# A fused retention and mixture-of-experts kernel: attention in blocks of two head pairs, half a batch ahead, with all its casts on GpSimd

## The chip, the core and the metric

The kernel runs on one core of a Trainium2 chip. A core has five engines with queues of their own: TensorE (PE, matrix products, with weight loads PEld beside them), VectorE (DVE), ScalarE (ACT), GpSimd (POOL) and SyncE (SP, which here only issues DMA). The metric is the device time of one execution in microseconds (us), the median of the runs given. Times inside an execution come from one profiled execution, counted from the start of its span.

## What is computed

Per batch (8), head (8), with 576 positions and a head dimension of 64, a retention attention: scores of q and k, multiplied by a decay that is zero above the diagonal, times v. Its output, transposed to 4608 tokens of 512 features, goes through four experts of two layers, mixed by normalised weights.

```python
scores = scale * np.matmul(q, k.transpose(0, 1, 3, 2))
Dmat = np.where(rel >= 0, gamma[:, None, None] ** rel[None, :, :], 0.0)
ret = scores * Dmat[None, :, :, :]
x = np.matmul(ret, v)                      # then to [B*S, H*D]
...
p = domain_probs / (domain_probs.sum(-1, keepdims=True) + 1e-09)
for e in range(E):
    h = np.maximum(x @ w1[e], 0.0)
    out += p[:, e:e + 1] * (h @ w2[e])
```

## The kernel before

**Tokens and experts.** The 4608 tokens are worked in nine tiles of 512 (`t` = 0 to 8). A tile has 16 up groups (`up_group`, L352: eight matmuls of 512 columns into one PSUM tile `ph`, then on DVE relu times the mixing weight `pB` into `h`, L364; in tile 0 on ACT) and, from tile 1 on, 14 down products (`Down.product`, L433: 16 matmuls of 256 columns each into `pd`). The products are a Strassen-Winograd scheme for two halves (s = 0, 1) of the tile: seven products each, in the order 1, 4, 2, 5, 6, 3, 7. They need the sums s1, s2, s4 and the difference in `h` (`Down.sums`, L421 to L431), which DVE makes from SBUF operands, each in two instructions. s1 is read by product 5, s2 by 6, s4 by 3 and the difference by 7. Tile 0 has plain down products.

**Order.** The schedule is manual: each engine runs its instructions in program order. In each tile a counter `n` goes through 30 slots: 16 up groups and 14 products. After each one, `run(slots, n)` issues what was put into that slot. So a slot fixes only the place in each engine's queue; an engine other than PE may run ahead to it.

**Attention.** Batch b needs tokens 576 b to 576 b + 575. Its first 512 positions are worked in four head pairs (`Pair`, L233), its last 64 in `Rem` (L302). Decay is folded into q and k: k and q are multiplied by tables while they are cast to bf16 (k on DVE L241, q on GpSimd L245, v copied on ACT L249), then k and q are transposed by DMA from SP's queue (L254). `scores` (L268) makes 8 matmuls with 64 contraction rows (array tiling 64x128) into `s`, and DVE multiplies by the triangle into `sT` (L276). `kv` (L257) makes 8 matmuls with 64 output rows (128x64) into `kvp`, which ACT copies to the block-diagonal `sbd` (L266). `values` (L280) makes 3 full-array products of `sbd` and q (L284), then the scores and kv of the following pair, then 8 products of v and `sT` (L291, 128x64), and ACT copies `o` to the token tile `xt` (L298). For batches 2 to 7, `attention` puts this into the tile before the batch: casts in slots 2, 7, 12, 18, heads in slots 7, 11, 17, 22, 27. Batches 0 and 1 are worked another way (`Unit`) in and before tile 0.

**Buffers.** All PSUM tiles come from one ring of four buffers (L64), taken in turn. `raw1`, the f32 load of a pair, has one buffer: the next load waits until the casts have read it. `bfs` has two sets (pairs p and p + 2 share one), `sbd` one.

**Queues.** SP issues in order: the two transposes of a pair, the six loads of the next (`load_pair`, L73), the remainder's five loads (`load_rem`), the output stores (L470, L486). GpSimd issues in order: the loads of next tile's `pB` (L222, in up groups 3, 7, 11, 15, each after DVE's last read of the old one), q casts (L245, L309) and the second half of an output sum (L485).

Of the kernel before, what the change touches and what calls it, by code (L numbers as in the profile page):

```python
# [9 lines left out]
FP32 = mybir.dt.float32  # L10
BF16 = mybir.dt.bfloat16
# [3 lines left out]
MULT = mybir.AluOpType.mult  # L15
# [8 lines left out]
def kernel(  # L24
# [41 lines left out]
    def ring_tile(name, shape, dt=FP32):  # L66
        return ring.tile(shape, dt, tag="ring", name=name)
# [5 lines left out]
    def load_pair(t, b, p, eng=nc.sync):  # L73
        for n, src in srcs:
            for j in range(2):
                eng.dma_start(out=t[n][:, :, j, :],
                              in_=src[b, 2 * p + j, 0:SM, :].rearrange("(c p) d -> p c d", p=C))
# [10 lines left out]
    bfr = {n: const.tile([128, NP, 2, D], BF16, name=f"bfr_{n}") for n, _ in srcs}  # L88
    raw1 = {n: const.tile([128, NC, 2, D], FP32, name=f"raw1_{n}") for n, _ in srcs}
    bfs = [{n: const.tile([128, NC, 2, D], BF16, name=f"bf{i}_{n}") for n, _ in srcs} for i in range(2)]  # L90
    q1 = const.tile([128, 2, 2, 4, D], BF16, name="q1")
    raw2 = const.tile([128, 3, 2 * NC * D], FP32, name="raw2")
    sbd = const.tile([128, NP, NC, 128], BF16, name="sbd")

    w1_sb = [const.tile([128, NDC, F], BF16, name=f"w1_{e}") for e in range(E)]
# [131 lines left out]
    def xt_of(t):  # L227
        if t not in xt:
            xt[t] = xpool.tile([128, NDC, NT], BF16, tag="xt", name="xt")
        return xt[t]  # L230


    class Pair:  # L233
        def __init__(self, b, p):
            self.b, self.p = b, p
            self.bf = bfs[p % 2]

        def cast(self, raw, n):
            p = self.p
            if n == "k":  # L240
                nc.vector.tensor_tensor(  # L241
                    self.bf["k"], raw["k"],
                    gk[:, :, 2 * p:2 * p + 2].unsqueeze(3).to_broadcast([128, NC, 2, D]), op=MULT)
            elif n == "q":
                nc.gpsimd.tensor_tensor(  # L245
                    self.bf["q"], raw["q"],
                    gq[:, :, 2 * p:2 * p + 2].unsqueeze(3).to_broadcast([128, NC, 2, D]), op=MULT)
            else:
                nc.scalar.activation(self.bf[n], raw[n], Copy)  # L249

        def trans_dma(self):
            self.qkT = atp.tile([128, 2, NC, C], BF16, tag="qkT", name="qkT")
            for i, n in ((1, "k"), (0, "q")):
                nc.sync.dma_start_transpose(  # L254
                    out=self.qkT[:, i, :, :], in_=self.bf[n][:, :, :, :].rearrange("p c h d -> p (c h d)"))

        def kv(self):  # L257
            kvp = ring_tile("kvp", [128, NC, D])
            for c in range(NC):
                for j in range(2):  # L260
                    nc.tensor.matmul(kvp[64 * j:64 * j + 64, c:NC, :], lhsT=self.bf["k"][:, c, j, :],  # L261
                                     rhs=self.bf["v"][:, c, j, :].unsqueeze(1).to_broadcast([128, NC - c, D]),
                                     start=(c == 0), stop=(c == NC - 1), skip_group_check=True)
            for j in range(2):
                r = slice(64 * j, 64 * j + 64)
                nc.scalar.activation(sbd[r, self.p, :, r], kvp[r, :, :], Copy)  # L266

        def scores(self):  # L268
            self.sT = atp.tile([128, 2, NC, C], BF16, tag="sT", name="sT")
            s = ring_tile("s", [128, 2, NC, C])  # L270
            for c in range(NC):
                for j in range(2):
                    r = slice(64 * j, 64 * j + 64)
                    nc.tensor.matmul(s[:, j, c, :], lhsT=self.qkT[r, 1, c, :], rhs=self.qkT[r, 0, c, :],  # L274
                                     start=True, stop=True)
            nc.vector.tensor_tensor(  # L276
                self.sT[:, :, :, :].rearrange("p j c t -> p (j c) t"), s[:, :, :, :].rearrange("p j c t -> p (j c) t"),
                tri[:, :].unsqueeze(1).to_broadcast([128, 2 * NC, C]), op=MULT)

        def values(self, following=None):  # L280
            b, p = self.b, self.p
            o = ring_tile("o", [128, SM])
            for c in range(1, NC):
                nc.tensor.matmul(o[:, c * C:(c + 1) * C], lhsT=sbd[:, p, c - 1, :], rhs=self.qkT[:, 0, c, :],  # L284
                                 start=(c == 1), stop=False, skip_group_check=True)
            if following is not None:
                following.scores()
                following.kv()
            for c in range(NC):
                for j in range(2):  # L290
                    nc.tensor.matmul(o[64 * j:64 * j + 64, c * C:(c + 1) * C], lhsT=self.bf["v"][:, c, j, :],  # L291
                                     rhs=self.sT[:, j, c, :], start=False, stop=(c == NC - 1), skip_group_check=True)
            n0 = b * S
            a = 0
            while a < SM:
                t = (n0 + a) // NT
                z = min(SM, (t + 1) * NT - n0)
                nc.scalar.activation(xt_of(t)[:, p, n0 + a - t * NT:n0 + z - t * NT], o[:, a:z], Copy)  # L298
                a = z


    class Rem:  # L302
        def __init__(self, b):
            self.b = b

        def cast(self, q_engine=nc.gpsimd):
            nc.vector.tensor_tensor(
                bfr["k"], rawr["k"], gkr[:, :].unsqueeze(2).unsqueeze(3).to_broadcast([128, NP, 2, D]), op=MULT)
            q_engine.tensor_tensor(  # L309
                bfr["q"][0:R], rawr["q"][0:R],  # L310
                gqr[0:R].rearrange("p (g j) -> p g j", j=2).unsqueeze(3).to_broadcast([R, NP, 2, D]), op=MULT)
            nc.scalar.activation(bfr["v"], rawr["v"], Copy)

        def alloc_trans(self):
            self.kT = atp.tile([128, NP, 128], BF16, tag="kTr", name="kTr", bufs=1)
# [333 lines left out]
    for u in range(NU):  # L649
# [10 lines left out]
        if u == NU - 2:  # L660
            warm(2)
    mixing_weights()
    raw1u = {n: raw1[n][:, :, :, :].rearrange("p c j d -> p (c j d)") for n in "kqv"}
    bf1 = [{}, {}]
    for g in range(2):
# [24 lines left out]
    load_w1(3)  # L690
    load_v(2)
    load_w2(3)
    early.close()
    hp = ctx.enter_context(tc.tile_pool(name="hp", bufs=1))
    h = hp.tile([128, E * NFC, NT], BF16, name="h")


    def attention(slots, b, cast_at, head_at):
        add = lambda i, f: slots.setdefault(i, []).append(f)
        xs = [Pair(b, p) for p in range(NP)]  # L700
        add(head_at[0], xs[0].scores)
        add(head_at[0], xs[0].kv)
        for p in range(NP):
            add(head_at[p + 1], lambda p=p: xs[p].values(xs[p + 1] if p + 1 < NP else None))
        for p, c in enumerate(cast_at):
            x = xs[p]
            add(c, lambda x=x: [x.cast(raw1, n) for n in "kqv"])
            add(c, x.trans_dma)
            if p + 1 < NP:
                add(c, lambda p=p: load_pair(raw1, b, p + 1))  # L710
            elif b + 1 < B:
                add(c, lambda: load_pair(raw1, b + 1, 0))

    def remainder(slots, b, at):
        add = lambda i, f: slots.setdefault(i, []).append(f)
# [9 lines left out]
    def run(slots, i):  # L725
        for f in slots.get(i, []):
            f()
# [41 lines left out]
            run(slots, n)  # L769
            n += 1  # L770

    HK = KH // 2
    for t in range(1, n_nt):
        slots = {i - 32: f for i, f in slots.items() if i >= 32} if t == 1 else {}
        d = [Down(h, t, s) for s in range(2)]
        add = lambda i, f: slots.setdefault(i, []).append(f)
        for s in range(2):
            for i, which in enumerate((1, 2, 4, 3)):
                for lo in (0, KH // 2):
                    add(16 + 7 * s + i, lambda s=s, which=which, lo=lo: d[s].sums(which, lo, lo + KH // 2))  # L780
        if t == 1:
            rem_next = Rem(1)
            add(0, rem_next.cast)
            add(0, rem_next.trans_dma)
            add(5, rem_next.scores)
            add(7, rem_next.values)
        elif t < B:
            add(2, rem_next.scores)
            add(4, rem_next.values)
        if t + 1 < B:  # L790
            rem_next = Rem(t + 1)
            add(21, lambda t=t: load_rem(t + 1))
            add(26, rem_next.cast)
            add(26, rem_next.trans_dma)
        if t + 1 < B:
            attention(slots, t + 1, (2, 7, 12, 18), (7, 11, 17, 22, 27))
        run(slots, -1)
        n = 0
        for e in range(E):
            for i in range(4):  # L800
                up_group(h, t, e, i)
                run(slots, n)
                n += 1
        for s in range(2):
            for m in (1, 4, 2, 5, 6, 3, 7):
                d[s].product(m)
                run(slots, n)
                n += 1
# [30 lines left out]
```

## Time and profile before

| | us |
|---|---|
| median of 3 runs (541.2 to 541.92) | 541.65 |
| the profiled execution | 541.59 |
| its span | 539.9 |
| tile 1 to tile 2, first up matmul to first up matmul (84.42 to 142.69) | 58.27 |
| tiles 2 to 6, each | 57.81 |
| h eviction, DVE L364, mean | 1.222 |
| sT, DVE L276, mean | 1.217 |
| k cast, DVE L241, mean (lowest 0.677) | 0.907 |
| q cast, GpSimd L245, mean | 1.108 |
| v copy, ACT L249, mean | 0.629 |

The profile names instructions by line, engine, operation and the tiles they write and read. A group line has count, busy time, mean ns of one, and the idle time of the engine just before. In timelines a trailing bracket is idle time before the row and what released it. "Chain" is the sequence of work that ended last, followed back from the last instruction.

### The profile page before, as it was taken

The page shows a single profiled execution, that of the slowest core. Times are in us where ns is not written, and L with a number is a line of the kernel's source. Part 1 is how long each engine was busy: PE and PEld are TensorE (multiplying, and loading weights), DVE is VectorE, ACT ScalarE, POOL GpSimd, SP SyncE. Part 2 cuts the span into 40 slices and gives each one's busy share as a digit, 9 for nine tenths or more (in the row PEclk, how much of TensorE's full clock was granted, in tenths as well). Part 3 has the DMA queues.
Part 4 walks back from the last instruction along what each step waited for, and adds up shares of the span by engine and source line. Part 5 has one row for each costly group of instructions (what it writes and reads, how often), then busy time and mean ns, then how long its engine had stood idle before and what let it go on. Part 6 is the DMA issues. An engine that isn't in the chain of part 4 may idle for free.

```text
span 539.9 us, 10290 instructions
## 1 busy us (share of the span) xinstructions
PE 528.9 (98%) x4278; PEld 340.8 (63%) x4318; DVE 366.4 (68%) x484; ACT 112.3 (21%) x255; POOL 92.8 (17%) x126
## 2 busy tenths in 40 slices
PE   8999999999999999999999999999999999999997
PEld 4444554568645884488547864687458844884486
DVE  5425669987488757875689658764886677557764
ACT  4633551122111320223022111131112200000010
POOL 5734001120211120211112111202111100010000
PEclk9999999999999999999999999999999999999999
DMA  9999957865266725555287517652654211110001
GB/s 239 207 211 250 227 133 178 154 148 118 84 119 133 166 77 109 136 111 141 73 158 123 146 55 137 157 138 85 105 132 117 80 42 39 41 41 21 0 27 53
DMA packets 145119, 63.56 MB, mean 118 GB/s; under 512 B 124240, under 2 KB 135888, under 8 KB 145072
## 3 DMA queue, kind: packets, MB, share of 16 engines
q1 hardware_dynamic: 134752, 43.50, 35.9%
q0 software_dynamic: 10176, 19.27, 16.3%
q8 instruction: 34, 0.56, 0.5%
q10 hardware_dynamic: 144, 0.13, 0.1%
q14 instruction: 13, 0.11, 0.1%
HBM read 53.56 MB, written 9.51 MB: 117 GB/s over the span
## 4 chain that ended last, share of the span: by engine, by line
PE 92%; DVE 4%; ACT 1%; issue 1%; DMA 1%; SPq 0%; DVEq 0%
PE ph L358 45%; PE pd L450 37%; PE po L377 4%; DVE h L364 2%; PE kvp L261 1%; PE s L274 1%; PE o L291 1%; ACT qkT L518 1%; DMA raw_0q<-in_q_dram 1%; PE o L284 1%; DVE sT L541 0%; PE kvp L558 0%; PE pt L516 0%; PE s L539 0%; PE o L602 0%
## 5 line engine op out<-in xcount | busy, mean ns | idle before, releaser
L358 PE MATMUL ph<-xt,w 128*128 128x512 bf16 x1118 | 252.5, 379 | 3.3 <-DVE h L364 1.4
L358 PEld LDWEIGHTS <-w 128*128 128x128 bf16 x1152 | 110.9, 98 | 129.6 <-issue 1.9
L364 DVE SCALAR_TENSOR_TENSOR h<-ph,pB 128x1024 bf16<-128x1024 f32 x128 | 155.9, 1222 | 51.1 <-PE ph L358 50.9
L450 PEld LDWEIGHTS <-h 128*128 128x128 bf16 x1024 | 99.2, 98 | 14.1
L450 PEld LDWEIGHTS <-s 128*128 128x128 bf16 x768 | 74.7, 98 | 9.1
L450 PE MATMUL pd<-wx,h 128*128 128x256 bf16 x512 | 61.3, 273 | 0.0
L450 PE MATMUL pd<-wx,s 128*128 128x256 bf16 x512 | 61.2, 273 | 0.0
L222 POOL DMA_DIRECT2D pB<-pd x28 | 15.9, 568 | 168.5 <-DVE h L364 136.8
L266 ACT ACTIVATE sbd<-kvp 64x256 bf16<-64x256 f32 x48 | 18.2, 379 | 105.6 <-PE kvp L261 105.3
L485 POOL TENSOR_TENSOR ob<-v,p 128x256 f32<-128x256 f32 x15 | 10.9, 727 | 146.9 <-DVE v L482 97.6
L245 POOL TENSOR_TENSOR bf_q<-raw_q,gq 128x512 bf16<-128x512 f32 x24 | 26.6, 1108 | 27.0 <-DMA raw_q<-in_q_dram 15.1
L276 DVE TENSOR_TENSOR sT<-s,tri 128x1024 bf16<-128x1024 f32 x24 | 29.2, 1217 | 2.1 <-PE s L274 2.1
L450 PE MATMUL pd<-t2w,s 128*128 128x256 bf16 x256 | 30.6, 273 | 0.0
L450 PE MATMUL pd<-t4w,h 128*128 128x256 bf16 x256 | 30.6, 273 | 0.0
L450 PE MATMUL pd<-t3w,h 128*128 128x256 bf16 x256 | 30.6, 273 | 0.0
L467 DVE TENSOR_TENSOR u<-pd,p 128x256 f32<-128x256 f32 x16 | 6.8, 425 | 33.7 <-PE pd L450 33.7
L377 PE MATMUL po<-wx,h 128*128 128x512 bf16 x124 | 28.4, 379 | 0.3 <-issue 0.2
L458 ACT ACTIVATE p<-pd 128x256 f32<-128x256 f32 x16 | 6.1, 384 | 92.8 <-PE pd L450 88.7
L469 DVE TENSOR_TENSOR oa<-pd,u 128x256 f32<-128x256 f32 x16 | 6.8, 425 | 23.7 <-PE pd L450 23.7
L431 DVE TENSOR_TENSOR s<-h,s 128x1024 bf16<-128x1024 bf16 x32 | 22.6, 747 | 0.0
L429 DVE TENSOR_TENSOR h<-h 128x1024 bf16<-128x1024 bf16 x32 | 22.2, 735 | 0.0
L249 ACT ACTIVATE bf_v<-raw_v 128x512 bf16<-128x512 f32 x24 | 15.1, 629 | 33.5 <-DMA raw_v<-in_v_dram 33.5
(147 smaller groups left out, 390.8 us busy)
## 6 DMA issues: line engine op xcount, KB each, us to landing
pB<-pd POOLq DMA_DIRECT2D x28, 256.0 KB, 3.9
raw_k<-in_k_dram SPq DMA_DIRECT2D x48, 128.0 KB, 2.7
raw_q<-in_q_dram SPq DMA_DIRECT2D x48, 128.0 KB, 3.2
raw_v<-in_v_dram SPq DMA_DIRECT2D x48, 128.0 KB, 4.0
wx<-in_moe_w_dram POOLq DMA_DIRECT2D x4, 1024.0 KB, 15.4
out_dram<-oa SPq DMA_DIRECT2D x16, 256.0 KB, 2.1
out_dram<-ob SPq DMA_DIRECT2D x15, 256.0 KB, 2.0
w<-in_moe_w_dram POOLq DMA_DIRECT2D x3, 1024.0 KB, 15.1
```

The costliest lines, as they stand in the source:

```text
L222: eng.dma_start(out=pB[t, e], in_=pd[e:e + 1, t * NT:(t + 1) * NT].to_broadcast([128, NT]))
L245: nc.gpsimd.tensor_tensor(self.bf["q"], raw["q"], gq[:, :, 2 * p:2 * p + 2].unsqueeze(3).to_broadcast([128, NC, 2, D]), op=MULT)
L249: nc.scalar.activation(self.bf[n], raw[n], Copy)
L266: nc.scalar.activation(sbd[r, self.p, :, r], kvp[r, :, :], Copy)
L276: nc.vector.tensor_tensor(self.sT[:, :, :, :].rearrange("p j c t -> p (j c) t"), s[:, :, :, :].rearrange("p j c t -> p (j c) t"), tri[:, : ...
L358: nc.tensor.matmul(ph[:, f, :], lhsT=w1_sb[e][:, dc, fc * 128:(fc + 1) * 128], rhs=x[:, dc, :], start=(dc == 0), stop=(dc == NDC - 1))
L364: nc.vector.scalar_tensor_tensor(h[:, fk:fk + 2, :], ph, 0.0, pB[t, e][:, :].unsqueeze(1).to_broadcast([128, 2, NT]), op0=MAX, op1=MULT)
L377: nc.tensor.matmul(po[:, g, :], lhsT=h[:, e * NFC + fc, ns * 128:(ns + 1) * 128], rhs=wx[e // 2][:, (e % 2) * NFC + fc, :, :].rearrange("p ...
L429: nc.vector.tensor_tensor(h[:, l, self.b], h[:, l, self.a], h[:, l, self.b], op=SUB)
L431: nc.vector.tensor_tensor(self.alloc("s4")[:, l], h[:, r, self.a], self.s2[:, l], op=SUB)
L450: mm = nc.tensor.matmul(dst, lhsT=src[:, kk, tok], rhs=rhs(c), start=(start and c == 0), stop=(c == KH - 1), skip_group_check=True)
L485: nc.gpsimd.tensor_tensor(self.ob[:, HF:Dm], self.v, self.p5, op=ADD)
```

## The change

Batches 2 to 7 are worked by `Duo`, two head pairs at a time, and `block(new, old)`: the kv of the new two pairs, then the values of the old two (v and `sT` products first, then the `sbd` products), then the scores of the new two. So within a block the array tilings are 128x64, 128x128 and 64x128, in this order. The `sbd` copies and the `xt` copies take two pairs at once.

All casts of these batches, and of the remainders of batches 1 to 7, are on GpSimd: k, q, v in this order. In tile 0 the remainder's v cast moves from ACT to DVE. k and q are transposed into tiles of their own (two buffers for kT, four for qT), and v has four buffers, so that a pair's v and q outlive the next half batch.

The slots of tiles 1 to 8 are now one list, numbered through (30 per tile). Batches 2, 3 and 4 have places of their own; from batch 5 on, with g = 30 (b - 3): casts at g+3, +8, +15, +21, blocks at g+13 and g+33, remainder loads at +17, casts at +27, scores at +36, values at +38. Batch 2 has no old values in its first block, its last values stand alone in slot 27, and batch 3's first block again has no old ones; the last values of batch 7 are at slot 163, in tile 6. As before, tiles 7 and 8 have no head pairs; the remainder of batch 7 is now in tile 6.

Two buffers of tile 0 (`q1`, `raw2`) move into a pool that is closed after tile 0; the new tiles take its place.

```diff
+    class Duo:
...
+        def cast(self, p):
+            for n, eng, g in (("k", nc.gpsimd, gk), ("q", nc.gpsimd, gq)):
+                eng.tensor_tensor(bfs[p % 2][n], raw1[n],
+                                  g[:, :, 2 * p:2 * p + 2].unsqueeze(3).to_broadcast([128, NC, 2, D]), op=MULT)
+            nc.gpsimd.tensor_copy(bv[p], raw1["v"])
+            self.kT[p] = dpl.tile([128, NC, C], BF16, tag="kT", name="kT", bufs=2)
+            self.qT[p] = dpl.tile([128, NC, C], BF16, tag="qT", name="qT", bufs=4)
+            for t, n in ((self.kT[p], "k"), (self.qT[p], "q")):
+                nc.sync.dma_start_transpose(out=t, in_=bfs[p % 2][n][:, :, :, :].rearrange("p c h d -> p (c h d)"))
...
         def kv(self):
+            kvp = ring_tile("kvp", [128, 2, NC, D])
+            for i, p in self.pairs():
+                for c in range(NC):
+                    for j in range(2):
+                        nc.tensor.matmul(kvp[64 * j:64 * j + 64, i, c:NC, :], lhsT=bfs[p % 2]["k"][:, c, j, :],
+                                         rhs=bv[p][:, c, j, :].unsqueeze(1).to_broadcast([128, NC - c, D]),
+                                         start=(i == 0 and c == 0), stop=(c == NC - 1), skip_group_check=True)
             for j in range(2):
                 r = slice(64 * j, 64 * j + 64)
-                nc.scalar.activation(sbd[r, self.p, :, r], kvp[r, :, :], Copy)
+                nc.scalar.activation(sbd[r, self.ps, :, r], kvp[r], Copy)
...
+        def values(self):
+            o = ring_tile("o", [128, 2, SM])
+            for i, p in self.pairs():
+                for c in range(NC):
+                    for j in range(2):
+                        nc.tensor.matmul(o[64 * j:64 * j + 64, i, c * C:(c + 1) * C], lhsT=bv[p][:, c, j, :],
+                                         rhs=self.sT[p][:, j, c, :], start=(c == 0), stop=False, skip_group_check=True)
+            for i, p in self.pairs():
+                for c in range(1, NC):
+                    nc.tensor.matmul(o[:, i, c * C:(c + 1) * C], lhsT=sbd[:, p, c - 1, :], rhs=self.qT[p][:, c, :],
+                                     start=False, stop=(c == NC - 1), skip_group_check=True)
...
+    def block(new, old):
+        if new is not None:
+            new.kv()
+        if old is not None:
+            old.values()
+        if new is not None:
+            new.scores()
...
-        def cast(self, q_engine=nc.gpsimd):
-            nc.vector.tensor_tensor(
+        def cast(self, engine=nc.gpsimd):
+            engine.tensor_tensor(
                 bfr["k"], rawr["k"], gkr[:, :].unsqueeze(2).unsqueeze(3).to_broadcast([128, NP, 2, D]), op=MULT)
-            q_engine.tensor_tensor(
+            engine.tensor_tensor(
...
-            nc.scalar.activation(bfr["v"], rawr["v"], Copy)
+            engine.tensor_copy(bfr["v"], rawr["v"])
...
+    NS = 30
+    slots = {i - 32: f for i, f in slots.items() if i >= 32}
+    rem1 = Rem(1)
+    for at, f in ((0, rem1.cast), (0, rem1.trans_dma), (5, rem1.scores), (7, rem1.values)):
+        add(at, f)
+    old = None
+    for b in range(2, B):
+        g = NS * (b - 3)
+        cast_at, block_at, rem_at = {
+            2: ((1, 8, 13, 17), (13, 22), (14, 20, 25, 28)),
+            3: ((22, 27, 32, 37), (32, 42), (34, 40, 45, 47)),
+            4: ((42, 47, 52, 57), (52, 62), (53, 59, 65, 68)),
+        }.get(b, ((g + 3, g + 8, g + 15, g + 21), (g + 13, g + 33), (g + 17, g + 27, g + 36, g + 38)))
+        duos = [Duo(b, d) for d in range(2)]
+        for d in range(2):
+            if b == 3 and d == 0:
+                add(27, lambda old=old: block(None, old))
+                old = None
+            add(block_at[d], lambda new=duos[d], old=old: block(new, old))
+            old = duos[d]
+        for p, at in enumerate(cast_at):
+            add(at, lambda d=duos[p // 2], p=p: d.cast(p))
+            if p + 1 < NP:
+                add(at, lambda b=b, p=p: load_pair(raw1, b, p + 1))
+            elif b + 1 < B:
+                add(at, lambda b=b: load_pair(raw1, b + 1, 0))
...
+    add(NS * 5 + 13, lambda old=old: block(None, old))
```

More of the change, by code (lines that the diff above doesn't have):

```diff
@@ L90 @@
     bfs = [{n: const.tile([128, NC, 2, D], BF16, name=f"bf{i}_{n}") for n, _ in srcs} for i in range(2)]
-    q1 = const.tile([128, 2, 2, 4, D], BF16, name="q1")
-    raw2 = const.tile([128, 3, 2 * NC * D], FP32, name="raw2")
     sbd = const.tile([128, NP, NC, 128], BF16, name="sbd")
@@ L230, in xt_of @@
         return xt[t]
[L233 to L240, printed above, removed]
-                nc.vector.tensor_tensor(
[L242 to L255, printed above, removed]
-        def kv(self):
[L258 to L263, printed above, removed]
@@ new lines, with __init__, pairs @@
+    class Duo:
+        def __init__(self, b, d):
+            self.b, self.d = b, d
+            self.ps = slice(2 * d, 2 * d + 2)
+            self.qT, self.kT, self.sT = {}, {}, {}
+        def cast(self, p):
[7 more added lines that the diff above has]
+                nc.sync.dma_start_transpose(out=t, in_=bfs[p % 2][n][:, :, :, :].rearrange("p c h d -> p (c h d)"))
+        def pairs(self):
+            return enumerate((2 * self.d, 2 * self.d + 1))
+        def kv(self):
+            kvp = ring_tile("kvp", [128, 2, NC, D])
[5 more added lines that the diff above has]
+                                         start=(i == 0 and c == 0), stop=(c == NC - 1), skip_group_check=True)
@@ L264, in kv @@
             for j in range(2):
                 r = slice(64 * j, 64 * j + 64)
-                nc.scalar.activation(sbd[r, self.p, :, r], kvp[r, :, :], Copy)
+                nc.scalar.activation(sbd[r, self.ps, :, r], kvp[r], Copy)
         def scores(self):
[L269 to L293, printed above, removed]
+            for i, p in self.pairs():
+                sT = self.sT[p] = atp.tile([128, 2, NC, C], BF16, tag="sT", name="sT")
+                s = ring_tile("s", [128, 2, NC, C])
+                for c in range(NC):
+                    for j in range(2):
+                        r = slice(64 * j, 64 * j + 64)
+                        nc.tensor.matmul(s[:, j, c, :], lhsT=self.kT[p][r, c, :], rhs=self.qT[p][r, c, :],
+                                         start=True, stop=True)
+                nc.vector.tensor_tensor(
+                    sT[:, :, :, :].rearrange("p j c t -> p (j c) t"), s[:, :, :, :].rearrange("p j c t -> p (j c) t"),
+                    tri[:, :].unsqueeze(1).to_broadcast([128, 2 * NC, C]), op=MULT)
@@ new lines, in values @@
+        def values(self):
+            o = ring_tile("o", [128, 2, SM])
+            for i, p in self.pairs():
+                for c in range(NC):
+                    for j in range(2):
+                        nc.tensor.matmul(o[64 * j:64 * j + 64, i, c * C:(c + 1) * C], lhsT=bv[p][:, c, j, :],
+                                         rhs=self.sT[p][:, j, c, :], start=(c == 0), stop=False, skip_group_check=True)
+            for i, p in self.pairs():
+                for c in range(1, NC):
+                    nc.tensor.matmul(o[:, i, c * C:(c + 1) * C], lhsT=sbd[:, p, c - 1, :], rhs=self.qT[p][:, c, :],
+                                     start=False, stop=(c == NC - 1), skip_group_check=True)
+            n0 = self.b * S
@@ L297, in values @@
                 z = min(SM, (t + 1) * NT - n0)
-                nc.scalar.activation(xt_of(t)[:, p, n0 + a - t * NT:n0 + z - t * NT], o[:, a:z], Copy)
+                nc.scalar.activation(xt_of(t)[:, self.ps, n0 + a - t * NT:n0 + z - t * NT], o[:, :, a:z], Copy)
                 a = z
+    def block(new, old):
[5 more added lines that the diff above has]
+            new.scores()
     class Rem:
@@ L304, in __init__ @@
             self.b = b
-        def cast(self, q_engine=nc.gpsimd):
-            nc.vector.tensor_tensor(
+        def cast(self, engine=nc.gpsimd):
+            engine.tensor_tensor(
                 bfr["k"], rawr["k"], gkr[:, :].unsqueeze(2).unsqueeze(3).to_broadcast([128, NP, 2, D]), op=MULT)
-            q_engine.tensor_tensor(
+            engine.tensor_tensor(
                 bfr["q"][0:R], rawr["q"][0:R],
                 gqr[0:R].rearrange("p (g j) -> p g j", j=2).unsqueeze(3).to_broadcast([R, NP, 2, D]), op=MULT)
-            nc.scalar.activation(bfr["v"], rawr["v"], Copy)
+            engine.tensor_copy(bfr["v"], rawr["v"])
         def alloc_trans(self):
@@ L662 @@
     mixing_weights()
+    early.close()
+    hp = ctx.enter_context(tc.tile_pool(name="hp", bufs=1))
+    h = hp.tile([128, E * NFC, NT], BF16, name="h")
+    first = ctx.enter_context(ExitStack())
+    fpool = first.enter_context(tc.tile_pool(name="fpool", bufs=1))
+    q1 = fpool.tile([128, 2, 2, 4, D], BF16, name="q1")
+    raw2 = fpool.tile([128, 3, 2 * NC * D], FP32, name="raw2")
     raw1u = {n: raw1[n][:, :, :, :].rearrange("p c j d -> p (c j d)") for n in "kqv"}
@@ L692 @@
     load_w2(3)
[L693 to L712, printed above, removed]
     def remainder(slots, b, at):
@@ L770 @@
             n += 1
-    HK = KH // 2
+    first.close()
+    dpl = ctx.enter_context(tc.tile_pool(name="dpl", bufs=1))
+    bv = [bfs[0]["v"], bfs[1]["v"]] + [dpl.tile([128, NC, 2, D], BF16, name=f"v{i}") for i in range(2)]
+    NS = 30
[7 more added lines that the diff above has]
+        cast_at, block_at, rem_at = {
[3 rows of a table added]
+        }.get(b, ((g + 3, g + 8, g + 15, g + 21), (g + 13, g + 33), (g + 17, g + 27, g + 36, g + 38)))
[12 more added lines that the diff above has]
+                add(at, lambda b=b: load_pair(raw1, b + 1, 0))
+        rem = Rem(b)
+        add(rem_at[0], lambda b=b: load_rem(b))
+        for at, f in ((rem_at[1], rem.cast), (rem_at[1], rem.trans_dma), (rem_at[2], rem.scores), (rem_at[3], rem.values)):
+            add(at, f)
+    add(NS * 5 + 13, lambda old=old: block(None, old))
     for t in range(1, n_nt):
-        slots = {i - 32: f for i, f in slots.items() if i >= 32} if t == 1 else {}
         d = [Down(h, t, s) for s in range(2)]
-        add = lambda i, f: slots.setdefault(i, []).append(f)
         for s in range(2):
@@ L779 @@
                 for lo in (0, KH // 2):
[L780 to L798, printed above, removed]
+                    add(NS * (t - 1) + 16 + 7 * s + i,
+                        lambda s=s, which=which, lo=lo, d=d: d[s].sums(which, lo, lo + KH // 2))
+        n = NS * (t - 1)
         for e in range(E):
```

## The prediction

> **What bounds the kernel now.** I read the page first: busy shares, then the chain that ended last.
>
> ```profile
> PE 528.9 (98%) x4278; PEld 340.8 (63%) x4318; DVE 366.4 (68%) x484; ACT 112.3 (21%) x255; POOL 92.8 (17%) x126
> ...
> PE 92%; DVE 4%; ACT 1%; issue 1%; DMA 1%; SPq 0%; DVEq 0%
> ```
>
> TensorE (PE) is busy 98% and carries 92% of the chain, so a change pays only if it shortens PE's own sequence or PE's waits. Next, the table of stretches, one token tile each (us, then busy time of PE, PEld, DVE, ACT, POOL):
>
> ```profile
> 373.93:431.74 57.81, 57.40 (x469) 38.53 (x473) 41.78 (x51) 10.64 (x27) 9.69 (x11) 1.00 0.48 107
> 484.40:536.20 51.80, 51.69 (x348) 34.15 (x349) 33.05 (x41) 2.30 (x6) 2.18 (x3) 1.00 0.05 19
> ```
>
> A tile with one batch's attention between its expert matmuls (tiles 1 to 6) takes 57.81, one without 51.80: attention costs about 6 us a tile, six times. Clock 1.00 in both. Then the chain within one tile (start, length, what):
>
> ```profile
> 349.84 0.17 PE o L284 x3
> 350.01 0.33 PE s L274 x8
> 350.34 0.40 PE kvp L261 x8
> 350.74 0.23 PE o L291 x8
> 350.96 8.84 PE pd L450 x80
> ...
> 369.76 0.17 PE o L284 x3
> 369.93 0.34 PE o L291 x8
> 370.28 1.74 PE pd L450 x15
> ```
>
> The same eight o matmuls of L291 take 0.23 directly after kvp (same array tiling, 128x64) and 0.34 directly after L284 (full array): 0.11 is the price of the change of tiling. It shows at each one: s takes 0.33, though eight half-array matmuls side by side stream 4x128 columns, 0.22 at 0.0539 per 128 columns (16 matmuls of 512 in 3.45 elsewhere in the chain): 0.11 over; kvp 0.40 against 0.27: 0.13; the 80 pd behind it 8.84 against 8.73 (24.45/224 each): 0.11. I take 0.12 a change. Last, PE's timeline where it sits idle:
>
> ```profile
> 397.10 1.67 PE L358 MATMUL ph<-xt,w 128*128 128x512 bf16 x6 [0.20 <-DVE h L364]
> ```
>
> The four PSUM ring buffers set this: o, s, kvp follow ph 11, so ph 12 needs the buffer of ph 11, whose eviction (1.22) has just begun. The list of waits has six such, 1.4 us together.
>
> **PE, tiling changes.** The matmuls stay the same in number and shape; only their order changes. Before, per batch: scores and kv alone: 3 changes (into s, into kv, back); three pairs with a following one: 3 each (full to s, s to kv, o back); the last: 2. That is 14, times 6 = 84. After: block = kv of two pairs, then o of the old two (same tiling), sbd products (full), scores, back: 4 changes, eight or so per batch. Counted out with the special cases: 3+4+2 for batch 2 (its last values alone in slot 27), 3+4 for batch 3, 8 each for 4 to 7, and 2 for the last values: 50. Removed 34 x 0.12 = 4.1 us, all of it on the path, since PE waits for nothing there.
>
> **PE, the ring wait.** A block takes kvp, o, s, s from the ring. The first s needs the buffer of the ph before last, the second that of the last ph (DVE done at 1.3 after the block starts, PE there after kv 0.54+0.12, o 0.43, sbd 0.32+0.12, s 0.22+0.12: 1.9). Covered; the 1.4 goes. What is late next: the following ph needs kvp's buffer, evicted by two ACT operations of 64x512. No such row; 64x256 takes 0.38 and the L298 row of 128x448 0.54, so 0.59 each: 0.76 after the start plus 1.2 = 1.95, PE arrives at 2.05 to 2.1. Between 0 and 0.1 a block over 11 blocks with scores: 0 to 1.1 us; I take 0.3, since it should just fit. In slot-22 blocks the buffer is pd's, free 0.9 after its last product. sT (two of 1.22 on DVE) and xt are read a block or more later: covered by ten slots.
>
> **DVE and ACT lose the casts** (24 x 0.68 or more, and 24 x 0.63): off the path, credited nothing.
>
> **GpSimd gains them.** Uncontended rows: a k or q cast 1.04, a v copy 0.61 (L503): 2.7 a pair instead of one 1.04; 4 pairs and a remainder add some 9 us to 9.7 busy of 57: room. Queued behind a cast that waits for its load: the pB loads (needed a tile later) and the ob sum of L485 (its p5 is rewritten four products later, 7 us). Neither reaches PE. The Trainium skill, "GPSIMD Engine Reference", "4.1 Engine selection", speaks against this: elementwise work belongs on VectorE, GpSimd being about twice as slow for two inputs. Rows: 1.04 against 0.68, 1.5 times. By the rule a pair is 2x1.36+0.61 = 3.3 (an estimate), by the row 2.7; both fit, so the sum is the same.
>
> **The port.** DVE's Strassen sums read two SBUF operands, and so do the casts:
>
> ```profile
> 233.11 1.28 DVE L427 TENSOR_TENSOR s<-s,h 128x1024 bf16<-128x1024 bf16 x2
> ...
> 235.91 1.66 DVE L431 TENSOR_TENSOR s<-h,s 128x1024 bf16<-128x1024 bf16 x2
> ```
>
> ```profile
> 235.37 1.04 POOL L245 TENSOR_TENSOR bf_q<-raw_q,gq 128x512 bf16<-128x512 f32 x1 [1.68 <-DMA raw_q<-in_q_dram]
> ```
>
> (GpSimd's row is quoted from its own timeline.) The sums that started under the cast took 0.38 more, the cast kept its 1.04. "SBUF — State Buffer", "SBUF: two separate sides", calls it an exclusive lock, the later one blocked for the whole instruction. If bandwidth were shared, a cast would stretch too and cost DVE perhaps a half; by the lock each meeting costs DVE what is left of the cast, up to 1.04. I sum with the lock. First half of a steady tile: DVE frees after ph 15; pair 2 casts then. With the engines taking turns, s1 is done 2.3 later (due at 3.9), s2 at 5.2 (due 5.7), s4 6.5 (7.4), s3 7.8 (9.2). Second half, against pair 3, the ob sum and the remainder cast (6.1 of GpSimd together): s1 at 2.8 (due 5.2), s2 5.8 (7.0), s4 8.7 (8.7, second half 9.6), s3 10 (10.5). No wait, with half a us to spare. The h evictions read PSUM and one SBUF operand; beside casts they keep 1.22.
>
> **SP's queue.** Cycle of a pair now (start, length):
>
> ```profile
> 150.07 1.20 SPq L254 DMA_TRANSPOSE qkT<-bf_k  x1
> 151.36 1.23 SPq L254 DMA_TRANSPOSE qkT<-bf_q  x1
> 152.64 1.12 SPq L76 DMA_DIRECT2D raw_k<-in_k_dram  x2
> 153.81 1.44 SPq L76 DMA_DIRECT2D raw_q<-in_q_dram  x2
> 155.34 1.00 SPq L76 DMA_DIRECT2D raw_v<-in_v_dram  x2
> ```
>
> The two transposes and six loads hold SP 6.3 us, and ACT could copy v only at 159.69, when its load was in. After the change: k cast 1.04, k transpose (q casts beside it), q transpose, k load in at 1.04+2.6+1.1+2.7 = 7.4 after the cast began, v at about 10.8. So a pair's k cast can follow the last one's by 7.4 to 8, against five slots of 1.73 or 1.75 (8.7, 8.9 with blocks). Two pairs are ready, transposed (2.4 to land), 13 us after the first cast; its block comes ten slots, 17 us, later: 4 to spare. With a remainder load between (five issues of 0.63) 16: 1 to 3.5 to spare in tiles 1 to 3. Output stores wait behind transposes at most some 3 us; their buffers are due a half tile later. Earlier code (tile 0) loads and computes as before; the remainder's v there moves to DVE, about 0.5, beside PE's work.
>
> **Sum.** 541.59 is the profiled execution (span 539.9, 1.7 around it). 4.1 + 1.4 - 0.3 = 5.2: 536.4, span 534.7; the median, 541.65, is 0.06 above it: 536.4. Steady tiles go from 57.8 to about 56.9.
>
> **Rivals.** (a) The operands come late: if the pair cycle is 9.5, not 8 (single issues of v took up to 2.5 for 1.0), 0.7 a pair is lost over the nine or so pairs of slots 17 to 57: 6, less 3.5 spare = 2.5: 539. For it: SP is nearly full there; against: the raw loads landed in 2.7 to 4.0 with DMA at half load. (b) Slower: GpSimd keeps the port against the sums in the second half of the tile. Then s1's second part waits for all 6.1: done 8.3 after the first product, due 6.1: 2.2 late, 1.6 if the remainder's v copy doesn't meet it; in five tiles (1 to 5) 8 us: 544.4. It decides from 1.3 a tile (6.3 in all). For it: my spare is half a us; against: before, engines took turns (two DVE sums beside one cast lost 0.86, not more). (c) The order doesn't do what it says, because the price is in the short matmuls and not in the changes: only the 1.4 goes: 540.2. Against: the 0.23 and 0.34 of one and the same group.
>
> **Chances.** Forecast 0.62 (534.8 to 538), (a) 0.14, (b) 0.14, (c) 0.10. Range 534.8 to 540.6: from changes at 0.13 with no new wait to (a) and (c) whole; it leaves out most of (b). A measurement here tells about 0.2% (1.1 us) from no change. Faster: 0.61 + 0.11 of (a) + 0.06 of (c) + 0.02 of (b) = 0.80; same: 0.01 + 0.02 + 0.04 + 0.02 = 0.09; slower: 0.01 of (a) and 0.10 of (b) = 0.11.
>
> **What would show it.** Right: tiles 4 and 5 at 56.8 to 57.1; a block as kvp x16, o x16, o x6, s x16 of about 2.1 us; no ph wait for h; tiles 7 and 8 unchanged. Wrong: PE idle before pd, released by DVE s or h sums (b); before kvp or s, released by POOL or a transpose (a); o behind kvp no shorter than before (c); ph idle behind ACT sbd: the kvp eviction.

## The result, and the profile after

The changed kernel took 536.76 us (median of 4, 536.19 to 537.38) against 541.78 for the kernel before in the same measurement: a ratio of 0.9901, 95% interval 0.9873 to 0.993. The forecast was 536.4, faster. Its profiled execution took 536.36, span 534.7 (534.7 was forecast). A second measurement gave 536.34 against 541.49: 0.9904 (0.989 to 0.9917).

Busy shares and the chain by engine, from the page of the changed kernel:

```profile
PE 526.9 (99%) x4318; PEld 339.2 (63%) x4318; DVE 361.3 (68%) x454; ACT 87.3 (16%) x175; POOL 145.1 (27%) x188
...
PE 95%; DVE 2%; ACT 1%; DMA 1%; issue 0%; SPq 0%; DVEq 0%
```

GpSimd has 52 us more work, ACT 25 less, DVE only 5 less, though 22 us of the pairs' k casts left it: its sums got longer. PE's share of the chain rose from 92 to 95%, which is what a kernel looks like when PE's waits go and nothing takes their place. The same table of stretches as before the change, cut at the first up matmul of a tile (tiles 1, 2, 3 and 6; the last three columns are PE's granted clock, the DMA share and GB/s):

```profile
84.42:141.98 57.56, 57.40 (x485) 38.65 (x484) 43.57 (x50) 7.62 (x16) 24.17 (x29) 1.00 0.73 160
141.98:200.34 58.36, 58.27 (x506) 39.32 (x504) 41.86 (x47) 8.43 (x17) 23.19 (x27) 1.00 0.76 160
200.34:257.22 56.88, 56.88 (x474) 38.27 (x472) 42.51 (x45) 7.23 (x15) 21.50 (x24) 1.00 0.63 142
...
370.99:426.65 55.66, 55.66 (x442) 37.27 (x440) 35.57 (x43) 6.05 (x13) 3.64 (x6) 1.00 0.12 39
```

A steady tile takes 56.88, not 57.81, and PE is busy in all of it. Tile 2 takes 0.55 more than before and tile 6 takes 2.15 less: that is attention moved forward, three blocks in tile 2, and in tile 6 only one full block and the short one. Tile 1 begins at 84.42 in both traces, so nothing was won before it; tiles 1 to 6 together take 5.1 less, which is nearly all of the 5.2.

The chain within a steady tile:

```profile
341.02 0.68 PE kvp L255 x16
341.70 0.45 PE o L280 x16
342.15 0.44 PE o L284 x6
342.59 0.55 PE s L269 x16
343.14 3.56 PE ph L359 x16
```

Each group carries its change of tiling once, for twice as many matmuls: o directly behind kvp 0.45 (two times 0.23, no change), L284 0.44 (six matmuls stream 0.32), s 0.55 (0.43). The list of PE's waits has one row left for ph (second line), where the kernel before had 1.4 us in six (first line):

```profile
PE ph L358 <- DVE h L364: 1.4, 6, 0.4
PE ph L359 <- DVE h L365: 0.2, 1, 0.2
```

### The profile page after: what moved, and what is told of

Same layout as the page of the kernel before. It is cut to its first block, busy times and chain, and to the rows that moved or that the text cites. A ratio compares the mean times of both kernels' runs of the same rounds, so it can differ in the third digit from the quotient of the medians.

```text
span 534.7 us, 10343 instructions
## 1 busy us (share of the span) xinstructions
PE 526.9 (99%) x4318; PEld 339.2 (63%) x4318; DVE 361.3 (68%) x454; ACT 87.3 (16%) x175; POOL 145.1 (27%) x188
## 4 chain that ended last, share of the span: by engine, by line
PE 95%; DVE 2%; ACT 1%; DMA 1%; issue 0%; SPq 0%; DVEq 0%
PE ph L359 47%; PE pd L451 37%; PE po L378 5%; PE kvp L255 1%; PE o L280 1%; PE s L269 1%; PE o L284 1%; ACT qkT L519 1%; DMA raw_0q<-in_q_dram 1%; DVE h L365 0%; DVE sT L542 0%; PE kvp L559 0%; PE s L540 0%; PE o L603 0%; PE w L138 0%; PE pt L517 0%
## 5 line engine op out<-in xcount | busy, mean ns | idle before, releaser
L239 POOL TENSOR_TENSOR bf_k<-raw_k,gk 128x512 bf16<-128x512 f32 x24 | 26.1, 1086 | 30.9 <-DMA raw_k<-in_k_dram 19.3
L260 ACT ACTIVATE sbd<-kvp 64x512 bf16<-64x512 f32 x24 | 14.2, 593 | 121.5 <-PE kvp L255 121.2
L428 DVE TENSOR_TENSOR s<-s,h 128x1024 bf16<-128x1024 bf16 x32 | 30.3, 988 | 0.0
L432 DVE TENSOR_TENSOR s<-h,s 128x1024 bf16<-128x1024 bf16 x32 | 26.0, 852 | 0.0
L426 DVE TENSOR_TENSOR s<-h 128x1024 bf16<-128x1024 bf16 x32 | 24.6, 810 | 0.0
```

What stands on the lines that cost most here:

```text
L239: eng.tensor_tensor(bfs[p % 2][n], raw1[n], g[:, :, 2 * p:2 * p + 2].unsqueeze(3).to_broadcast([128, NC, 2, D]), op=MULT)
L260: nc.scalar.activation(sbd[r, self.ps, :, r], kvp[r], Copy)
L426: nc.vector.tensor_tensor(self.alloc("s1")[:, l], h[:, l, self.b], h[:, r, self.b], op=ADD)
L428: nc.vector.tensor_tensor(self.alloc("s2")[:, l], self.s1[:, l], h[:, l, self.a], op=SUB)
L432: nc.vector.tensor_tensor(self.alloc("s4")[:, l], h[:, r, self.a], self.s2[:, l], op=SUB)
```

## Experiments

A ratio below is to the kernel before, on the same chip. The yardstick for variants is the changed kernel: 536.3 to 536.8.

### More changes of tiling, same matmuls

```diff
             for i, p in self.pairs():
                 for c in range(NC):
...
-            for i, p in self.pairs():
                 for c in range(1, NC):
                     nc.tensor.matmul(o[:, i, c * C:(c + 1) * C], lhsT=sbd[:, p, c - 1, :], rhs=self.qT[p][:, c, :],
...
```

> The changed kernel, but in each block's values the v products and the sbd products of the first old pair come before those of the second, so the array tiling goes 128x64, full, 128x64, full instead of 128x64, full: two more changes of tiling in each of the 12 values, 24 in all; the same matmuls. Theory (each change of tiling costs PE 0.11 to 0.12 us and nothing hides it): +2.6 to +2.9 us on the changed kernel, about 539.5, the values of a block 1.1 us instead of 0.9 in the trace. Rival C (the price lies in the short matmuls, not in the changes): 536.8, no difference.

Measured: 539.15 (538.82 to 539.38), ratio 0.9956 (0.9945 to 0.9968). Its chain, where the changed kernel has x16 and x6:

```profile
343.06 0.68 PE kvp L255 x16
343.74 0.23 PE o L280 x8
343.96 0.27 PE o L283 x3
344.24 0.34 PE o L280 x8
344.58 0.27 PE o L283 x3
```

The first o, behind kvp, takes 0.23, the second, behind the full array, 0.34. A steady tile takes 57.34: 0.45 more (mean of tiles 3 to 5) for four more changes, 0.113 each; 24 of them give 2.7, measured 2.4 to 2.8. The price lies in the changes; rival (c) falls.

### Fewer changes: sbd products first

`values_carried` holds the sbd products, `values_own` the v products; kvp keeps its place in the ring. (Here and below the lines `if new is not None` and `if old is not None` are left out.)

```diff
     def block(new, old):
+        new.kv_alloc()
+        old.values_carried()
         new.kv()
-        old.values()
+        old.values_own()
         new.scores()
```

> The changed kernel, with the block's order sbd products (full array, as the expert matmuls before them), kv, v products, scores: three changes of tiling instead of four in the ten blocks that have old and new pairs (the other blocks keep theirs), 10 fewer. The kvp tile still comes first in the PSUM ring, but kv runs 0.32 us later in the block, so its eviction by ACT (two of 0.59) ends about 2.3 us after the block's start, and PE wants the buffer at about 2.0. Theory: -1.2 us from the changes, given back as a wait of the next ph for ACT's sbd copy of 0.2 to 0.3 in 7 or 8 blocks (+1.5 to +2.4): 537 to 538. If the ring doesn't matter: 535.6. Rival C: 536.8 with no wait.

Measured: 538.93 (538.39 to 539.35), 0.9953 (0.9941 to 0.9965): 2.2 to 2.6 above the changed kernel, more than expected. The list of waits:

```profile
PE ph L370 <- ACT sbd L263: 2.4, 8, 0.4
...
PE pd L462 <- ACT sbd L263: 0.7, 2, 0.4
```

All ten blocks wait, 0.3 each, 3.1 in all. Ten changes are gone and their price comes back more than double, as a wait for the kvp buffer. So the changed kernel's order has a second effect: kv at the front gives the eviction its time. In the changed kernel ACT ends it at 342.94, and the next ph starts at 343.07:

```profile
341.74 1.20 ACT L260 ACTIVATE sbd<-kvp 64x512 bf16<-64x512 f32 x2 [8.93 <-PE kvp L255]
343.07 3.19 PE L359 MATMUL ph<-xt,w 128*128 128x512 bf16 x14
```

### The same, with the eviction on two engines

```diff
-                nc.scalar.activation(sbd[r, self.ps, :, r], kvp[r], Copy)
+                if j == 0:
+                    nc.scalar.activation(sbd[r, self.ps, :, r], kvp[r], Copy)
+                else:
+                    nc.vector.tensor_copy(sbd[r, self.ps, :, r], kvp[r])
```

> The same order as in the run with sbd products first (10 fewer changes of tiling than the changed kernel), and the kvp eviction split: one half on ACT, the other on DVE, side by side. Theory: both halves are done about 1.9 us after the block's start, before PE wants the buffer; the saved changes stay: 535.5 to 535.9, a version faster than both kernels. DVE has 24 operations of about 0.65 less than it had before the change for k casts, so its triangle products end by 4.4 us, in time. Rival C: 536.8.

Measured: 540.01 (539.66 to 541.83), 0.9972 (0.9962 to 0.9981): slower than one engine. DVE's row in one block:

```profile
288.04 0.69 DVE L266 CAST sbd<-kvp 64x512 bf16<-64x512 f32 x1 [0.41 <-ACT sbd L264]
```

DVE waited for ACT's half, so the two ran one after the other, and DVE's is the slower (0.69 against 0.59). My expectation had them side by side. With the order between the halves lifted (they write different partitions):

> As the run with sbd products first and the kvp eviction split between ACT and DVE, with the order between the two halves lifted (they write different partitions; in that run DVE waited for ACT in each block). DVE is free of the last h eviction 1.3 us after the block's start, so its half ends at 2.0, where PE wants the buffer: waits of ph for sbd fall from 0.4 to 0.1 or less a block, and the time from 540.0 to 535.7 to 536.7. If the waits stay at 0.3 to 0.5, the eviction's start and not its sequence sets them.

Measured: 536.1 (535.91 to 538.23), 0.9908 (0.9893 to 0.9923): 3.9 less than with the order kept, within the expected range, but no better than the changed kernel. Its DVE timeline shows why:

```profile
340.74 1.22 DVE L376 SCALAR_TENSOR_TENSOR h<-ph,pB 128x1024 bf16<-128x1024 f32 x1 [0.50 <-PE ph L370]
341.99 0.69 DVE L262 CAST sbd<-kvp 64x512 bf16<-64x512 f32 x1
```

The copy stands behind the last h eviction, ends at 342.68, and ph starts at 342.74: a steady tile takes 56.87. The change saved at the block's start (its first matmul follows ph without the 0.09 that kvp needs in the changed kernel) is spent at its end (0.10).

### Fewer changes, with kv still in front

```diff
         new.kv()
-        old.values()
+        old.values_own()
         new.scores()
+        old.values_carried()
```

> The changed kernel with the block's order kv, v products, scores, sbd products: tilings 128x64, 64x128, full, and the full array stays for the expert matmuls that follow; three changes instead of four in ten blocks, 10 fewer, and kv still at the front, so that its eviction starts as early as in the changed kernel. Theory: -1.0 to -1.2 us from the changes (0.10 each by the interleaved run), less a wait of up to 0.1 a block for the kvp eviction, since the block ends 0.1 us sooner: 535.6 to 536.4, faster than both kernels. If the saved change only turns into a wait for the eviction (PE ph behind ACT sbd, 0.1 in each of ten blocks): 536.7.

> The changed kernel again, unchanged, on the same chip as its variants, as their yardstick: 536.3 to 537.4, 0.990 of the kernel before.

Measured side by side: 535.76 (535.29 to 536.94) against the changed kernel's 536.34 (536.08 to 536.36); ratios 0.9901 (0.9886 to 0.9917) and 0.9904 (0.989 to 0.9917). It was measured once more:

> The version with the order kv, v products, scores, sbd products once more, for its interval: its first medians lay 0.6 us below the changed kernel's, and its profiled span 0.8 to 1.1 below. If ten changes at 0.10 are gone and nothing waits for it: a ratio to before of 0.988 to 0.990, 535 to 536.2. If the gain was chance: 0.9904, 536.4.

535.58 (535.24 to 535.7), 0.9879 (0.9862 to 0.9895). Both its medians lie below both of the changed kernel's, though the intervals of the ratios overlap in part. The traces agree with each other: a steady tile is 56.75 in both, 56.88 in both traces of the changed kernel; from the first up matmul of tile 1 to the end both take 0.6 less (449.7 against 450.3); and no ph waits for ACT. The gain is 0.13 a tile, 0.065 a change and not 0.11. Its chain:

```profile
340.08 0.68 PE kvp L255 x16
340.76 0.45 PE o L280 x16
341.21 0.59 PE s L269 x16
341.80 0.44 PE o L287 x6
```

s now takes 0.59, not 0.55: the missing 0.04. In this order the scores come earlier in the block, and their second half (the ninth of the sixteen matmuls) takes the ring buffer of the last ph. DVE empties that buffer here until 341.34:

```profile
340.12 1.23 DVE L370 SCALAR_TENSOR_TENSOR h<-ph,pB 128x1024 bf16<-128x1024 f32 x1 [0.50 <-PE ph L364]
```

In the single records of the trace the ninth s starts at 341.40, 0.076 after the eighth, where it follows by 0.053 in the changed kernel; the change out of s, from its last matmul to the next group's first, takes 0.148 in both. All eight full blocks that stand among up groups show this; the two that stand among down products don't, and there s comes without delay. So the saved change pays its 0.11 here too, and 0.04 of it goes to the ring, too short for the list of waits. This is the fastest version, by 0.6 to 1.2 us from the changed kernel, and 6 from before.

### The casts alone

The kernel before, with all these casts on GpSimd:

```diff
-                nc.vector.tensor_tensor(
+                nc.gpsimd.tensor_tensor(
                     self.bf["k"], raw["k"],
...
-                nc.scalar.activation(self.bf[n], raw[n], Copy)
+                nc.gpsimd.tensor_copy(self.bf[n], raw[n])
```

> The kernel before, in its own order and slots, with all casts of batches 2 to 7 (k, q, v, and the remainders) on GpSimd. My theory (the relief of DVE and ACT by itself is worth nothing): 541.2 to 542.0. Rival D (the relief is a good part of the gain): 537 to 540. Should the operands come late, since a pair is used four slots after its cast and three casts in a row take 1.7 us longer: above 542, with PE waiting before s or kvp.

Measured: 541.6 (541.26 to 544.39), 0.9993 (0.9973 to 1.0013); steady tiles 57.81, as before, with the same 0.20 before ph. The relief of DVE and ACT by itself is worth nothing that shows (the interval leaves room for 1.5 us, the equal steady tiles for none); rival D falls.

### The order alone: the casts back on their engines

The remainders' k and v casts go back too.

> The changed kernel with its casts on the engines of before, in the new slots: k (pairs and remainders) on DVE, v on ACT, q on GpSimd. Theory (the gain is the blocks' order; the relief of DVE and ACT is off PE's path): 536.8 within 0.8, with perhaps short waits of ph where a k cast stands in DVE's queue before an eviction of h. Rival D (the gain is the relief of DVE and ACT): back towards before, 540 to 541.5.

```diff
-            for n, eng, g in (("k", nc.gpsimd, gk), ("q", nc.gpsimd, gq)):
+            for n, eng, g in (("k", nc.vector, gk), ("q", nc.gpsimd, gq)):
...
-            nc.gpsimd.tensor_copy(bv[p], raw1["v"])
+            nc.scalar.activation(bv[p], raw1["v"], Copy)
```

Measured: 544.43, from 541.78 to 547.39; 1.0062 (1.0038 to 1.0085). Slower than before, and spread wide. Both of my expectations were wrong: it is neither "no difference" nor a return to the time before, but slower than that. PE waited 3.7 and 1.3 us before a product, for ACT's copy out of the pd bank. Each engine alone:

> The changed kernel with only the v copies (pairs and remainders) back on ACT; k and q stay on GpSimd. In the run with all engines of before ACT's v copy, placed ahead in the queue, stood waiting for its load (37.6 us in 7 waits), and behind it ACT's copy of a product out of the pd bank, for which PE waited 3.7 and 1.3 us. Theory V (that wait is the whole loss): the same waits of PE pd for ACT oa, 541 to 546, and varying from run to run with the arrival of the loads. Theory K (the k casts on DVE do it): 536.8.

> The changed kernel with only the k casts (pairs and remainders) back on DVE; q and v stay on GpSimd. Theory V: 536.8 to 538, since DVE's k casts wait for loads too, but were not seen to hold up PE in the run with all engines of before. Theory K: 541 or more, with PE waiting for h, s or oa of DVE.

v on ACT: 539.89 (539.25 to 541.37), 0.9962 (0.9946 to 0.9979). k on DVE: 541.96 (540.94 to 544.75), 1.0005 (0.9987 to 1.0023). Theory V was only a part, K the larger one. ACT's timeline with v, in tile 1:

```profile
122.53 0.63 ACT L241 ACTIVATE v<-raw_v 128x512 bf16<-128x512 f32 x1 [6.14 <-DMA raw_v<-in_v_dram]
123.07 0.37 ACT L462 ACTIVATE oa<-pd 128x256 f32<-128x256 f32 x1
```

DVE's with k:

```profile
121.48 0.69 DVE L239 TENSOR_TENSOR bf_k<-raw_k,gk 128x512 bf16<-128x512 f32 x1 [4.39 <-DMA raw_k<-in_k_dram]
```

The cast of batch 2's fourth pair stands in slot 17, before its load is in. On ACT it holds the copy oa behind it, on DVE the sum s2, and PE waits for these (here with v on ACT; with k on DVE the wait for s2 is 2.01):

```profile
123.49 1.91 PE L451 MATMUL pd<-t2w,s 128*128 128x256 bf16 x16 [2.28 <-ACT oa L462]
```

On GpSimd the same v copy starts just as late, and nothing that PE needs stands behind it. In the changed kernel's trace:

```profile
122.35 0.61 POOL L241 CAST v<-raw_v 128x512 bf16<-128x512 f32 x1 [3.35 <-DMA raw_v<-in_v_dram]
```

Tile by tile it is clear: with k on DVE, tiles 1 and 2 take 60.84 and 60.25 instead of 57.56 and 58.36; with v on ACT 60.01 and 59.24; from tile 3 on both take 56.88, the same as the changed kernel. The waits in PE's list come to 3.3 (k) and 3.0 (v) of the 5.2 and 3.3 that tiles 1 and 2 lose; what the rest of k's is was not traced. So the casts' engine is what allows the early slots of batches 2 to 4, and matters nowhere else.

### How near the edge it is

```diff
+            for _ in range(2):
                 for n, eng, g in (("k", nc.gpsimd, gk), ("q", nc.gpsimd, gq)):
...
                 nc.gpsimd.tensor_copy(bv[p], raw1["v"])
```

> The changed kernel with every cast of a pair done twice on GpSimd (k, q, v, then again; the second writes the same values), which adds 2.7 us to each pair on GpSimd and to its cycle of cast, transpose and load. My prediction held that the cycle has little to spare in the tiles of batches 2 to 4 (7.4 to 8 us of 8.7) and the sums about half a us (the trace showed 1.1). If that is right: 546 to 556, PE first waiting before s or kvp for transposes or casts in tiles 1 to 3, and then before pd for DVE's sums in tiles 3 to 5. If both have wide room: 536.8 to 539.

Measured: 572.99 (570.3 to 575.14), 1.0561 (1.0519 to 1.0604). Far more than expected. Its list of PE's waits:

```profile
PE s L270 <- DMA qT<-bf_q: 11.1, 8, 2.8
PE kvp L256 <- POOL v L242: 3.6, 2, 2.0
...
PE pd L452 <- DVE s L427: 3.5, 2, 1.8
```

The order of the expectation holds: operands late first (from 111.9 on), sums later (325). The size doesn't: tiles 1 to 5 take 5.8, 11.3, 8.1, 4.8 and 4.1 more, 34 in all. The waits listed come to 26. Of the other 8, slower matmuls are about 6: PE's busy time in tiles 2 and 3 is 3.6 and 2.3 longer than in the changed kernel, and the granted clock is 0.95 and 0.97 there (1.00 in every tile of the changed kernel). It falls directly behind long waits, as in tile 2 behind the 2.8 us for qT that ends at 202.94 (the clock is the third number from the end):

```profile
199.70:203.00 3.30, 0.49 (x13) 0.32 (x13) 1.23 (x1) 1.59 (x3) 0.00 (x0) 1.00 1.27 100
203.00:206.50 3.50, 3.50 (x25) 2.51 (x25) 3.13 (x3) 0.00 (x0) 2.21 (x2) 0.57 1.28 257
```

Where the last 2 go stays open.

## Why the prediction was right, point by point

**Changes of tiling, 34 at 0.12 = 4.1: right in kind, 0.3 too high.** A steady tile lost 0.93. Six changes fewer at the 0.113 of the interleaved run are 0.68 of it; the rest is the ring wait. By that price the 34 are 3.8.

**The ring wait, 1.4: right as a sum, not in its parts.** The list counts idle time from the modelled ends of matmuls. By the starts, ph came 0.41 after the last o of a steady tile, where the same change from o to pd takes 0.15: the wait cost 0.26 (0.50 in tile 1), 1.8 in all. With the 0.68 above, 0.26 makes the 0.93. Two such waits stayed, 0.22 and 0.15 by the starts, in the first blocks of batches 2 and 3, which have no old values. I had worked the ring out for full blocks only; without o the next ph takes the buffer of the last ph, as before the change. The list shows only the first of them, as 0.16. So 1.4 went: 1.8 less 0.4.

**kvp's eviction, 0.3 taken of 0 to 1.1: nothing.** ACT started it 0.79 after the block and ended at 1.99; the estimate was 0.76 and 1.95. The spare of 0.13 is real, and small: a block in which kv came 0.43 later waited 0.3. (The blocks that could wait are the ten with old values, not 11.)

**Casts, credited nothing for leaving DVE and ACT: right against the kernel before** (541.6 with the casts moved alone), **incomplete as a reason.** I asked what their absence saves, not what their presence would cost in the new slots: 3.3 (v) and 5.4 us (k) by the side runs' medians, against the mean of the changed kernel's two. A forecast for the order alone would have been wrong by all of it.

**GpSimd and the port: right.** The DVE and GpSimd timelines of the first half of tile 4:

```profile
292.20 2.99 DVE L428 TENSOR_TENSOR s<-s,h 128x1024 bf16<-128x1024 bf16 x2
```

```profile
291.94 1.25 POOL L239 TENSOR_TENSOR bf_k<-raw_k,gk 128x512 bf16<-128x512 f32 x1
293.15 1.49 POOL L239 TENSOR_TENSOR bf_q<-raw_q,gq 128x512 bf16<-128x512 f32 x1
294.59 1.07 POOL L241 CAST v<-raw_v 128x512 bf16<-128x512 f32 x1
```

The two instructions of s2, 1.28 together (L427 before), took 2.99, the casts 1.25, 1.49 and 1.07 instead of 1.04, 1.04 and 0.61: the engines took turns, each waiting for the other, as summed with the exclusive port of the Trainium skill ("SBUF — State Buffer", "SBUF: two separate sides"). The ends alternate: k cast 293.19, first of s2 293.73, q cast 294.64, second of s2 295.19, v copy 295.66; each of the two ended 0.55 after the cast before it. That the casts stretched too, which I had named as a sign of shared bandwidth, comes of the same turns: each of these casts began while a sum was under way, while the cast quoted in the prediction, which kept its 1.04, began beside a triangle product, which reads PSUM. s2 was done 1.5 before PE's product 6 began at 296.64, and 1.0 before in the second half of that tile (307.84, 308.87); I had 0.5 of spare. Rival (b), GpSimd keeping the port, did not come; with twice the casts PE does wait for the sums, 1.8 at most (the doubled run).

**Operands, 3.5 us to spare in batch 2: right.** The fourth pair's v copy ended at 122.96, 3.3 before its block began at 126.26; its q transpose, issued at 122.56 with 2.4 to landing, was there about 3 before its scores at 128.07. Rival (a) is the one that decides first when a pair costs more on GpSimd.

**The sum, 5.2: 5.0 by the medians (5.15 in the second measurement), 5.2 by the profiles.** The terms as measured are 3.8 + 1.4 and nothing for kvp's eviction. The changes were put 0.3 too high and the reserve of 0.3 was not used: two small misses cancel, and that the forecast of the span came out to the tenth is luck. The range's lower end doesn't follow from the words beside it: 34 changes at 0.13 and the 1.4 are 5.8, which is 535.8 and not 534.8.

## What to carry to other kernels

When PE is busy 98%, look for what it does between matmuls: here each change of array tiling cost it about 0.11 us, and grouping the same matmuls by tiling, with half a batch of delay so that nothing in a group depends on the group before it, took away the changes. Count the ring buffers in program order for every kind of block, the short ones too: a saved change is worth less, or nothing, if the next buffer isn't free. And a cast placed ahead of its load belongs on an engine whose queue holds nothing that PE waits for; which engine is fastest at it is the smaller question.

## What the runs showed of the hardware that I had not expected

The price of a change of tiling was the same for every pair of tilings here, by the starts in the records of the changed kernel and of the fastest version. From the last matmul of a group to the first of the next it is 0.148 to 0.152 for 128x64 to full, full to 64x128, 128x64 to 64x128 and 64x128 to full, where matmuls inside these groups follow by 0.053 to 0.056; the second matmul comes another 0.01 late. The longer s of the fastest version is no dearer change but the wait for a ring buffer.

PE's granted clock fell in three stretches of the doubled run, each directly behind waits of PE: to 0.83 and 0.87 around 172.5 to 184 (waits of 2.0 and 0.4), to 0.57 from 203.0 to 206.5 (2.8), to 0.62 from 233.4 to 236.9 (2.5). A wait of 2.4 at 276.7 had no such fall (1.00 from 270 to 282). That waits bring the clock down is therefore likely, but they were not varied to show it.
